# Sliding-window attention and a squared-ReLU FFN: the tail pair moved, squares moved between engines, another order for the first two blocks

## The chip, the cores and the metric

The kernel runs on one core of one Trainium2 chip. The metric is the device time in microseconds of one execution; lower is better. Engines are named as the profile names them: PE (matmuls), DVE (vector), ACT (scalar), POOL (GpSimd) and SP (which only issues DMAs).

## The reference

Attention over 8 batches, 8 heads, 576 positions and a head size of 64, in which each position sees itself and the 63 before it, and behind it an FFN with a squared ReLU on the 4608 tokens:

```python
scores = scale * np.matmul(q, k.transpose(0, 1, 3, 2))
rel = pos[:, None] - pos[None, :]
mask = (rel >= 0) & (rel < 64)
attn = softmax(np.where(mask, scores, -1e9))
x = np.matmul(attn, v)                     # to [4608, 512]
h = np.maximum(x @ w_in, 0.0)              # w_in  [512, 2048]
out = h * h @ w_out                        # w_out [2048, 512]
```

Inputs and output are float32 in device memory.

## The kernel before

**Tiles, pairs, blocks.** Tokens are worked on in 36 tiles of 128, 18 pairs of tiles and 9 blocks of two pairs (512 tokens). A sequence of 576 positions is two pairs of 256 and a rest of 64. The rests of the eight sequences are put together into two special pairs, four rests in each: `TAILS` says which pair numbers these are, and `place` turns the other pairs into sequence and position. A tail pair is loaded by `fetch_tail` (L163): twelve DMAs on SP, the keys and values with the 64 positions ahead of each rest, so twice the bytes of a usual pair; two tiles of keys are transposed for it instead of one. A usual pair is loaded by `fetch_two` with six DMAs.

**One tile of attention.** `S_` makes the scores on PE (L425), `expo` the exponentials on ACT (L431), `keep` applies the mask on DVE as a minimum (L436), `V` multiplies with the values on PE (L448), `norm` divides on DVE (L456, L457). The result x is transposed to xT, by PE and a copy (`X`, `copy_xT`) for blocks 0 to 3, by DMA for later ones. Keys and queries of pairs 0 to 6 are transposed on PE (`T`, L373) and copied out of PSUM by `copy_kT` and `copy_qT`; those of later pairs by DMA (L397).

**The FFN of one block.** `UP(g, f)` (L526) makes one sixteenth of the hidden units of block g: four matmuls into a PSUM bank of `ps_up`, which has two buffers. ACT takes the relu out of the bank (L530), and the square into h2 is made on ACT from the relu alone (L533) if f is in `SQ_ACT`, else on DVE from the bank and the relu (L536). In blocks 0 and 1 the same is done by pairs: `U` (L498), `relu` (L506 on ACT, L508 on DVE), `square` (L517, L519). The output product of block 0 is plain (`O`, L574); that of the later blocks (`out_seven`) uses seven products of half blocks instead of eight (L614), with sums of halves of h2 on DVE (`hsum`, L602) and sums of the weights (`w_out_sum`, L555 to L561).

**What sets the order.** Every engine works its queue in the order in which the program issues. For blocks 0 and 1 that order is written out by hand in `FIRST`, a list of words: `fk`, `fq`, `fv`, `fw`, `fo` fetch keys, queries, values and weights; `kc`, `qc`, `vc` cast them; `vd` copies values to the tile with the halves exchanged; `Tk`, `Tq` transpose, `ck`, `cq` copy the transposed tiles; `w` scales w_in, `o` casts w_out; `S`, `e` (or `ea`, `eb` by halves), `m`, `V`, `n`, `X`, `x` are attention; `U`, `r`, `s` the up-projection of a pair, its relu and square; `O`, `oe`, `st` the output of block 0; `ws` the weight sums; `Wn` issues n matmuls that compute nothing and keep PE busy. A letter after the slash gives the engine (A for ACT, D for DVE, P for POOL) in place of the word's own.

From block 2 on, a stage g puts together the seven products of block g-1, the sixteen `UP` of block g, the attention of block g+1 and the loads of pairs 2g+4 and 2g+5, each with a place between 0 and 1 within the stage, and issues them sorted by it. `later(n, ...)` puts an instruction off by n steps.

Of the kernel before, what the change touches and what calls it, by code (L numbers as in the profile page):

```python
# [12 lines left out]
ALU = mybir.AluOpType  # L13


SQ_ACT = (0, 2, 4, 6, 8, 10, 12, 14)
FIRST = '''
fv3 fk0 fk1 W9 vc3 fq0 kc0/D kc1/A fq1 h0 vd3/D Tk0 W3 kc3/A kc2 fv1 ck0 Tk1 W8 qc0 qc1/D fv0 h2
ck1 Tq0 W11 fv2 cq0 qc2/A fw3 qc3/D S0 fw2 vc1/D fw1 S1 W5 ea0 fw0 vc0/D eb0 vd0/D ea1 vc2 vd1/D
V0 eb1 Tq1 vd2 n0 cq1/A V1 W3 n1 X0 W3 x0 X1 S3 x1/A w3.0 w3.3/A fq2 w3.1 S2 w3.2 ea3 eb3 U0.6 ea2  # L20
V3 eb2 U0.7 n3 w2.1/A w2.3/A w2.0 V2 w2.2 r0.6 X3 n2 U0.5 r0.7 s0.6/A s0.7 X2 U0.4 x2/A x3 w1.0/P
r0.5/D U1.4 r0.4 h4 s0.5 fk2 w1.3/A U1.7 w1.1/P r1.4/D s0.4/A U1.6 w1.2 s1.4/A r1.7/D U1.3 w0.3/A
w0.2 s1.7/A U1.2 w0.0 fv4 r1.6 w0.1 U1.5 r1.3 s1.6 r1.2 qc4 fv5 U0.2 r1.5 s1.2 qc5 s1.3/A s1.5 fk3
kc4 kc5/A Tq2 r0.2 Tk2 vc4 fq3 cq2/A U0.1 ck2/D vd4 U1.1 r0.1 fq4 s0.2 vc5 s0.1/A S4 r1.1/D S5 vd5
e4 U0.0 h6 e5 U0.3 kc7 m4 fv6 r0.0 m5 V4 s1.1/A qc7 fv9 V5 n4 r0.3 U1.0 qc6 s0.0/A n5 fq5 X4 qc8
qc9/A Tq3 x4 r1.0 kc6 X5 s0.3 Tq4 fv7 x5/A vc6 Tk3 s1.0 cq3/A U2.5 vd6 ck3/D fk4 cq4/A U2.0 r2.5/D
S7 r2.0/D S6 e7 U2.2 fv8 s2.5 fo0 vc9/A U2.7 s2.0 e6 vc7 m7 fo1 U2.1 vd7 fo2 r2.2 m6 fo3 U2.4 qc10
s2.2/A h8 r2.1/D qc11/A kc9 V7 V6 r2.7 n7 vc8 U2.3 s2.7/A vd9 n6 s2.1/A U2.6 r2.3 r2.4/D kc8 X7 X6
x7 Tq5 s2.4/A vd8 x6 Tk4 s2.3/A r2.6/D U3.7 ck4 s2.6 o2 U3.6 o0 cq5 r3.7 fv10 o1 s3.7/A S9 S8 r3.6
U3.0 s3.6/A U3.2 e9 r3.0/D o4 U3.4 o7 s3.0/A m9 o3 e8 U3.1 r3.2/D U3.3 s3.2/A m8 o10 r3.1 h10  # L30
r3.4/D O0.0 o5 fv15 s3.1 s3.4/A o6 V8 V9 o8/A O2.0 n9 o9/A fk5 O3.0 n8 o15 o12/A o14/A o11 fk6
O0.1 ws0.0 vc10/A ws0.1 X9 o13/A h12 O3.1 vd10 r3.3/D fv14 ws0.2 X8 O3.2 ws1.1 ws0.3 O0.2 kc10
kc11/A x9 ws1.0 s3.3/A O2.1 ws1.3 fv12 ws1.2 ws2.3 O3.3 x8 fq6 ws2.2 kc12 kc13/A Tk5 ws2.0 O2.2
vc15/A ws2.1 fv11 vc14/A ck5/D Tk6 O0.3 vd14 ck6 fv13 O2.3 oe0 st0 vc12 S11 vd15 oe2/D st2 S10 e11
U3.5 qc13 fkq14 qc12 e10 O1.0 m11 vc11 O1.1 r3.5 m10 vd11 Tq6 vc13 V10 cq6/A V11 vd12 n10 O1.2
fkq15 n11 O1.3 qc14 s3.5 X10 kc14 oe1 st1 X11 x10 oe3 st3 vd13 x11 kc15 qc15
'''


# [1 line left out]
def kernel(  # L41
# [10 lines left out]
    B, H, S, D = q.shape  # L52
    NT, DM = out.shape
    DFF = moe_w_in.shape[1]
    P = 128
    HP = H // 2
    NCK = NT // P
    TAILS = (8, 15)
    W_SCALE = 100.0
    OUT_SCALE = 1.0 / (W_SCALE * W_SCALE)  # L60
    BIG = 65504.0
# [24 lines left out]
    def later(n, fn):  # L86
        if n == 0:
            fn()
        else:
            put_off.append([n, fn])  # L90

    def tick():
        for e in list(put_off):
            e[0] -= 1
            if e[0] <= 0:
                put_off.remove(e)
                e[1]()
# [6 lines left out]
    def is_tail(i):  # L104
        return i // 2 in TAILS

    def place(i):

        p = i // 2 - sum(i // 2 > t for t in TAILS)
        return p // 2, p % 2 * 256 + i % 2 * P  # L110

    def tail_seq(i):

        return 4 * TAILS.index(i // 2) + i % 2 * 2

    def is_first(i):
        return not is_tail(i) and place(i)[1] == 0
# [147 lines left out]
    def copy(eng, out, in_, scale=1.0):  # L265
        if eng is nc.scalar:
            nc.scalar.activation(out=out, in_=in_, func=AF.Copy, scale=scale)  # L267
        elif scale == 1.0:
            eng.tensor_copy(out=out, in_=in_)  # L269
        else:  # L270
            eng.tensor_scalar(out=out, in0=in_, scalar1=scale, scalar2=None, op0=ALU.mult)
# [25 lines left out]
    def shift_v(i, eng=nc.gpsimd):  # L297
        v_ev, v_od, v_next = v_evs[i % NV], v_ods[i % NV], v_ods[(i + 1) % NV]
        copy(eng, v_od[64:P, :, 0:D], v_ev[0:64, :, 0:D])
        if i >= 2 * TAILS[0] and is_first(i):  # L300
            eng.memset(v_od[0:64, :, 0:D], 0.0)
# [9 lines left out]
    def xT_of(g):  # L311
        if g not in xTs:
            xTs[g] = xtp.tile([P, 4, DMC, P], FP16, name="xT", tag="xT")
        return xTs[g]
# [84 lines left out]
    def dma_k(p):  # L399
        if p in TAILS:  # L400
            for i in (2 * p, 2 * p + 1):
                kTs["tail", i] = attw.tile([P, 2, HP, P], FP16, name="kT", tag="kT", bufs=4)
                flip(kTs["tail", i][:].rearrange("p n a t -> p (n a) t"),
                     k16s["tail", i][:].rearrange("p n h d -> p (n h d)"))
        else:
            flip(kT_of(p)[:].rearrange("p a (n t) -> p (a n) t", n=2),
                 k16s[p][:].rearrange("p n h d -> p (n h d)"))
# [76 lines left out]
    def h2_of(g):  # L484
        if g not in h2s:
            h2s[g] = h2pool.tile([P, FFC, 512], FP16, name="h2", tag="h2")
        return h2s[g]
# [35 lines left out]
    def UP(g, f):  # L523
        hps = ps_up.tile([P, 512], FP32, name="hps", tag="ps_u")
        for c in range(DMC):
            nc.tensor.matmul(  # L526
                hps[:], w_in_sb[:, c, f * P:(f + 1) * P], xT_of(g)[:, :, c, :],
                start=(c == 0), stop=(c == DMC - 1))
        hrelu = hrp.tile([P, 512], FP32, name="hrelu", tag="hrelu")
        nc.scalar.activation(out=hrelu[:], in_=hps[:], func=AF.Relu)  # L530
        if f in SQ_ACT:

            later(2 if f == 0 else 0, lambda: nc.scalar.activation(  # L533
                out=h2_of(g)[:, f, :], in_=hrelu[:], func=AF.Square))
        else:
            nc.vector.scalar_tensor_tensor(  # L536
                out=h2_of(g)[:, f, :], in0=hps[:], scalar=0.0, in1=hrelu[:],
                op0=ALU.max, op1=ALU.mult)
        tick()
# [208 lines left out]
    def load(p, part):  # L748

        if p in TAILS:  # L750
            for nm in part:
# [42 lines left out]
    for g in range(2, NTB + 1):  # L794
        if g == 2:
            for k0 in range(0, KH, 2):
                w_out_sum(k0, 3)
        ev = even(out_seven(g - 1))
        if g < NTB:
            ev += [(0.05 + 0.95 * t, s) for t, s in even([lambda f=f: UP(g, f) for f in range(FFC)])]  # L800
        if g + 1 < NTB:
            ev += attention(g + 1)
            ev += loads(2 * g + 3)
        for _, s in sorted(ev, key=lambda e: e[0]):
            s()
# [32 lines left out]
```

The softmax here doesn't subtract the row's maximum and nothing guards it: scores larger than these inputs give would overflow.

## Time and profile before

| | us |
|---|---|
| median of 4 runs (lowest, highest) | 297.52 (296.29, 298.33) |
| the profiled execution | 297.73 |
| its span, first to last instruction | 295.9 |
| PE, DVE, ACT, POOL busy in it | 284.2, 218.0, 189.7, 118.1 |

The profile is of one execution. Its span is 1.8 us shorter than the time of the same execution. Busy times of PE are those of pipelined matmuls, so they overlap; a matmul's own time is longer than the distance to the next one. "Idle before" is the time an engine stood before an instruction, put down to what came last. Times on the timeline are counted from the first instruction.

### The profile page before, as it was taken

How to read it: one execution, taken by the hardware profiler on the slowest of the kernel's cores; microseconds unless marked ns; L12 is line 12 of the kernel's file. 1: busy time of each engine (PE TensorE's matmuls, PEld its weight loads, DVE VectorE, ACT ScalarE, POOL GpSimd, SP SyncE). 2: the span in 40 equal slices, each digit the busy share in tenths (PEclk: the TensorE clock that was granted, in tenths of full speed). 3: DMA queues.
4: the chain of work that ended last, by engine and by line, in shares of the span. 5: the costliest groups of instructions: out<-in, count | busy, mean ns of one | idle time of the engine just before them, and what ended most of it. 6: DMA issues, size and time to landing. Idle time of an engine off the chain costs nothing.

```text
span 295.9 us, 7475 instructions
## 1 busy us (share of the span) xinstructions
PE 284.2 (96%) x3042; PEld 196.7 (66%) x3042; DVE 218.0 (74%) x396; ACT 189.7 (64%) x300; POOL 118.1 (40%) x172
## 2 busy tenths in 40 slices
PE   4999999999989999999999999999999999999995
PEld 3668888755656666666666666666666566666684
DVE  4569798798889569685978587768776976645393
ACT  2688999885574756757675767575757575566500
POOL 2306979558506264545364626232366300000000
PEclk9999999999999999999999999999999999999999
DMA  7999999796699999868895999989999801300133
GB/s 216 297 381 312 305 285 370 215 267 163 183 187 237 190 279 214 191 154 253 197 218 132 232 209 200 149 195 199 228 227 313 120 3 35 144 0 2 71 106 109
DMA packets 151842, 57.64 MB, mean 195 GB/s; under 512 B 128256, under 2 KB 143616, under 8 KB 151808
## 3 DMA queue, kind: packets, MB, share of 16 engines
q1 hardware_dynamic: 151808, 57.16, 79.8%
q8 instruction: 24, 0.39, 0.5%
q14 instruction: 10, 0.08, 0.1%
HBM read 38.80 MB, written 9.44 MB: 163 GB/s over the span
## 4 chain that ended last, share of the span: by engine, by line
PE 73%; DVE 14%; ACT 7%; DMA 2%; issue 2%; SPq 0%; POOL 0%
PE hps L526 30%; PE opsC L614 9%; PE opsD L614 8%; PE hps L498 5%; PE opsA L614 5%; PE opsB L614 5%; DVE hs_all L602 4%; PE av L448 3%; ACT pm L431 2%; PE sc L425 2%; DVE pm L436 2%; DMA k_st<-in_k_dram 2%; ACT h L517 1%; DVE x_sb L457 1%; ACT hrelu L506 1%
## 5 line engine op out<-in xcount | busy, mean ns | idle before, releaser
L526 PE MATMUL hps<-xT,w_in_sb 128*128 128x512 f16 x448 | 112.8, 379 | 2.4 <-DVE h L536 2.4
L530 ACT ACTIVATE hrelu<-hps 128x512 f32<-128x512 f32 x112 | 66.7, 598 | 69.8 <-PE hps L526 68.7
L614 PEld LDWEIGHTS <-h 128*128 128x128 f16 x624 | 60.4, 98 | 20.7 <-issue 0.2
L526 PEld LDWEIGHTS <-w_in_sb 128*128 128x128 f16 x448 | 42.5, 98 | 35.0 <-issue 2.7
L536 DVE SCALAR_TENSOR_TENSOR h<-hps,hrelu 128x512 f16<-128x512 f32 x56 | 38.6, 690 | 29.2 <-ACT hrelu L530 28.8
L269 POOL COPY v_od<-v_ev 64x512 f16<-64x512 f16 x51 | 38.7, 758 | 7.3 <-ACT v_ev L267 3.5
L431 ACT ACTIVATE pm<-sc 128x1024 f16<-128x1024 f32 (+1 forms) x40 | 35.3, 937 | 3.6 <-PE sc L425 3.5
L533 ACT ACTIVATE h<-hrelu 128x512 f16<-128x512 f32 x56 | 35.2, 629 | 1.6
L614 PE MATMUL opsA<-w_out_sb,h 128*128 128x256 f16 x240 | 31.0, 273 | 0.0
L614 PE MATMUL opsD<-wb_all,h 128*128 128x256 f16 x240 | 30.9, 273 | 0.0
L614 PEld LDWEIGHTS <-hs_all 128*128 128x128 f16 x256 | 25.0, 98 | 8.6
L498 PE MATMUL hps<-xT,w_in_sb 128*128 128x256 f16 x256 | 30.2, 273 | 0.0
L498 PEld LDWEIGHTS <-w_in_sb 128*128 128x128 f16 x256 | 24.2, 98 | 3.0
L457 DVE TENSOR_TENSOR x_sb<-av,rden 128x512 f16<-128x512 f32 x36 | 24.9, 692 | 1.2
L436 DVE TENSOR_TENSOR pm<-pm,mask_inner 128x1024 f16<-128x1024 f16 x25 | 19.3, 772 | 6.5 <-ACT pm L431 6.4
L269 POOL CAST k<-kq_st 128x512 f16<-128x512 f32 x18 | 11.8, 657 | 27.1 <-DMA kq_st<-in_k_dram 26.6
L269 POOL CAST q<-kq_st 128x512 f16<-128x512 f32 x22 | 14.8, 673 | 18.4 <-DMA kq_st<-in_q_dram 18.3
L269 POOL CAST v_ev<-kq_st 128x512 f16<-128x512 f32 x16 | 11.2, 701 | 20.1 <-DMA kq_st<-in_v_dram 15.8
L636 DVE SCALAR_TENSOR_TENSOR osb_all<-opsD,u 128x512 f32<-128x512 f32 x14 | 9.7, 691 | 11.3 <-PE opsD L614 11.3
L614 PE MATMUL opsC<-w_out_sb,h 128*128 128x256 f16 x128 | 16.4, 273 | 0.0
L614 PE MATMUL opsB<-wb_all,hs_all 128*128 128x256 f16 x128 | 16.4, 273 | 0.0
L614 PE MATMUL opsC<-w_out_sb,hs_all 128*128 128x256 f16 x128 | 16.4, 273 | 0.0
(102 smaller groups left out, 379.3 us busy)
## 6 DMA issues: line engine op xcount, KB each, us to landing
kq_st<-in_k_dram SPq DMA_DIRECT2D x26, 256.0 KB, 3.7
kq_st<-in_v_dram SPq DMA_DIRECT2D x24, 256.0 KB, 3.8
out_dram<-osb_all SPq DMA_DIRECT2D x12, 512.0 KB, 4.1
kq_st<-in_q_dram SPq DMA_DIRECT2D x18, 256.0 KB, 4.4
v_st<-in_v_dram SPq DMA_DIRECT2D x16, 256.0 KB, 5.3
k_st<-in_k_dram SPq DMA_DIRECT2D x7, 512.0 KB, 5.6
q_st<-in_q_dram SPq DMA_DIRECT2D x7, 512.0 KB, 5.7
out_dram<-osb_all SPq DMA_DIRECT2D x11, 256.0 KB, 2.8
```

What stands on the lines that cost most here:

```text
L269: eng.tensor_copy(out=out, in_=in_)
L431: nc.scalar.activation(out=pms[i][:, part], in_=scs[i][:, part], func=AF.Exp, scale=1.0 / float(D) ** 0.5)
L436: nc.vector.tensor_tensor(out=pms[i][:, part], in0=pms[i][:, part], in1=mask[:].rearrange("p (o a) r -> p o (a r)", o=1) .to_broadcast([P, ...
L457: nc.vector.tensor_tensor(out=xs[i // 2][:, i % 2], in0=avs[i][:, :, :, 0:D], in1=rden[:].to_broadcast([P, 2, 4, D]), op=ALU.mult)
L498: nc.tensor.matmul(hps[:, f, :], w_in_sb[:, c, (2 * j + f) * P:(2 * j + f + 1) * P], xT_of(p // 2)[:, n0:n0 + 2, c, :], start=(c == 0), st ...
L526: nc.tensor.matmul(hps[:], w_in_sb[:, c, f * P:(f + 1) * P], xT_of(g)[:, :, c, :], start=(c == 0), stop=(c == DMC - 1))
L530: nc.scalar.activation(out=hrelu[:], in_=hps[:], func=AF.Relu)
L533: later(2 if f == 0 else 0, lambda: nc.scalar.activation(out=h2_of(g)[:, f, :], in_=hrelu[:], func=AF.Square))
L536: nc.vector.scalar_tensor_tensor(out=h2_of(g)[:, f, :], in0=hps[:], scalar=0.0, in1=hrelu[:], op0=ALU.max, op1=ALU.mult)
L602: nc.vector.tensor_tensor(out=Sh[i][:, ks], in0=x[:, ks], in1=y[:, ks], op=op)
L614: nc.tensor.matmul(rows_of(bank, m), a[:, kk, m * P:(m + 1) * P], w[:, kk], start=(first and kk == 0 and (m == 0 or bank in apart)), stop= ...
L636: nc.vector.scalar_tensor_tensor(out=dst, in0=banks[bank][:, ms], scalar=OUT_SCALE, in1=sums[add][:, ms], op0=ALU.mult, op1=ALU.add)
```

## The change

Three things change besides the list `FIRST`. The first tail pair becomes pair 10 (the first of block 5) instead of pair 8 (the first of block 4). `SQ_ACT` holds f=1 in place of f=2, so the square of f=1 goes to ACT and that of f=2 to DVE in every block from 2 on. In block 2, f=2 and f=9 are made on ACT too: ten squares there and six on DVE. The list `FIRST` holds the same steps in another order and with other engines for some of them; its `W` words add up to 43 matmuls in place of 42.

```diff
--- before.py
+++ after.py
@@ -13,27 +13,27 @@
 ALU = mybir.AluOpType
 
 
-SQ_ACT = (0, 2, 4, 6, 8, 10, 12, 14)
+SQ_ACT = (0, 1, 4, 6, 8, 10, 12, 14)
 FIRST = '''
-fv3 fk0 fk1 W9 vc3 fq0 kc0/D kc1/A fq1 h0 vd3/D Tk0 W3 kc3/A kc2 fv1 ck0 Tk1 W8 qc0 qc1/D fv0 h2
-ck1 Tq0 W11 fv2 cq0 qc2/A fw3 qc3/D S0 fw2 vc1/D fw1 S1 W5 ea0 fw0 vc0/D eb0 vd0/D ea1 vc2 vd1/D
-V0 eb1 Tq1 vd2 n0 cq1/A V1 W3 n1 X0 W3 x0 X1 S3 x1/A w3.0 w3.3/A fq2 w3.1 S2 w3.2 ea3 eb3 U0.6 ea2
-V3 eb2 U0.7 n3 w2.1/A w2.3/A w2.0 V2 w2.2 r0.6 X3 n2 U0.5 r0.7 s0.6/A s0.7 X2 U0.4 x2/A x3 w1.0/P
-r0.5/D U1.4 r0.4 h4 s0.5 fk2 w1.3/A U1.7 w1.1/P r1.4/D s0.4/A U1.6 w1.2 s1.4/A r1.7/D U1.3 w0.3/A
-w0.2 s1.7/A U1.2 w0.0 fv4 r1.6 w0.1 U1.5 r1.3 s1.6 r1.2 qc4 fv5 U0.2 r1.5 s1.2 qc5 s1.3/A s1.5 fk3
-kc4 kc5/A Tq2 r0.2 Tk2 vc4 fq3 cq2/A U0.1 ck2/D vd4 U1.1 r0.1 fq4 s0.2 vc5 s0.1/A S4 r1.1/D S5 vd5
-e4 U0.0 h6 e5 U0.3 kc7 m4 fv6 r0.0 m5 V4 s1.1/A qc7 fv9 V5 n4 r0.3 U1.0 qc6 s0.0/A n5 fq5 X4 qc8
-qc9/A Tq3 x4 r1.0 kc6 X5 s0.3 Tq4 fv7 x5/A vc6 Tk3 s1.0 cq3/A U2.5 vd6 ck3/D fk4 cq4/A U2.0 r2.5/D
-S7 r2.0/D S6 e7 U2.2 fv8 s2.5 fo0 vc9/A U2.7 s2.0 e6 vc7 m7 fo1 U2.1 vd7 fo2 r2.2 m6 fo3 U2.4 qc10
-s2.2/A h8 r2.1/D qc11/A kc9 V7 V6 r2.7 n7 vc8 U2.3 s2.7/A vd9 n6 s2.1/A U2.6 r2.3 r2.4/D kc8 X7 X6
-x7 Tq5 s2.4/A vd8 x6 Tk4 s2.3/A r2.6/D U3.7 ck4 s2.6 o2 U3.6 o0 cq5 r3.7 fv10 o1 s3.7/A S9 S8 r3.6
-U3.0 s3.6/A U3.2 e9 r3.0/D o4 U3.4 o7 s3.0/A m9 o3 e8 U3.1 r3.2/D U3.3 s3.2/A m8 o10 r3.1 h10
-r3.4/D O0.0 o5 fv15 s3.1 s3.4/A o6 V8 V9 o8/A O2.0 n9 o9/A fk5 O3.0 n8 o15 o12/A o14/A o11 fk6
-O0.1 ws0.0 vc10/A ws0.1 X9 o13/A h12 O3.1 vd10 r3.3/D fv14 ws0.2 X8 O3.2 ws1.1 ws0.3 O0.2 kc10
-kc11/A x9 ws1.0 s3.3/A O2.1 ws1.3 fv12 ws1.2 ws2.3 O3.3 x8 fq6 ws2.2 kc12 kc13/A Tk5 ws2.0 O2.2
-vc15/A ws2.1 fv11 vc14/A ck5/D Tk6 O0.3 vd14 ck6 fv13 O2.3 oe0 st0 vc12 S11 vd15 oe2/D st2 S10 e11
-U3.5 qc13 fkq14 qc12 e10 O1.0 m11 vc11 O1.1 r3.5 m10 vd11 Tq6 vc13 V10 cq6/A V11 vd12 n10 O1.2
-fkq15 n11 O1.3 qc14 s3.5 X10 kc14 oe1 st1 X11 x10 oe3 st3 vd13 x11 kc15 qc15
+fv3 fq0 h0 fk0 W9 fq1 qc0/A qc1 fk1 vc3 Tq0 W1 vd3/D kc0/A kc1/D fv0 cq0/A Tk0 W6 ck0/D qc3/A fv1
+fv2 S1 kc2/A S0 qc2/A vc0/D fw3 ea1 h2 vd0 kc3/D Tq1 W8 fw2 eb1 fw1 ea0 fw0 eb0 h4 Tk1 vc1/D vd1
+V0 W6 ck1 n0 cq1/A vc2 V1 X0 W6 n1 x0/A vd2/D X1 S2 x1/A S3 W7 fk2 w3.2 w3.1/A w3.0 ea2 w3.3 eb2
+U0.7 ea3 eb3 V2 U0.6 w2.0/A n2 w2.2/A w2.1 V3 r0.6 w2.3 X2 s0.6/A n3 U0.5 r0.7 x2 X3 s0.7/A U0.4
+x3 fq2 w1.0/A w1.1 U1.7 r0.5/D r0.4 s0.5 s0.4/A U1.6 r1.7 w1.2 w1.3 U1.4 fv4 r1.6 s1.7 U1.2 s1.6
+r1.4 kc4 w0.0/A w0.1 fv5 U1.3 w0.2/A s1.4 U1.5 r1.3 r1.2/D qc4 kc5/A U0.2 fq3 s1.2 s1.3/A w0.3 Tk2
+qc5/A fq4 r1.5/D U1.1 vc4 r0.2 s1.5 vd4 Tq2 ck2/D U0.1 cq2/A fk3 vc5 r1.1/D vd5 r0.1 S4 s0.2 S5
+fv7 e4 s1.1 qc7 U0.0 s0.1 e5 qc8 fv6 U1.0 m4 qc9 r0.0 m5 fv9 V4 r1.0 kc7 qc6/A n4 V5 s1.0/A U0.3
+n5 s0.0/A fq5 Tq3 kc6/A X5 X4 fk4 r0.3 x5 Tq4 vc6 x4 s0.3/A Tk3 h6 vd6 cq3 U2.5 ck3 fv13 U2.0 vc7
+cq4 r2.5 vc9 s2.5/A S7 S6 r2.0/D vd7 fv8 U2.7 e6 s2.0 fo0 U2.1 fo1 r2.7/D e7 kc9 m6 U2.4 fo2 vd9
+r2.1 fo3 m7 s2.1/A U2.6 s2.7/A kc8 r2.4/D qc11/A V7 qc10 V6 r2.6 h8 n7 vc13 U2.3 s2.6/A n6 s2.4/A
+X7 U2.2 x7/A r2.3 X6 Tk4 s2.3/A x6 Tq5 r2.2/D U3.0 fk5 cq5/A o3 s2.2 o1 U3.6 ck4/D r3.0 o0 U3.2
+vc8/A r3.6 vd8 U3.3 r3.2/D s3.0/A s3.2 S9 r3.3 vd13 S8 s3.6 e9 U3.5 s3.3 o6 U3.4 e8 m9 o5 U3.7
+o2/A fv14 m8 o4 r3.5 U3.1 r3.7/D s3.5/A o7 V9 r3.4 o9 V8 s3.7/A s3.4 o8 O0.0 fv10 o11/A o15 n9
+O1.0 o10/A o13 fk6 r3.1 X9 o14 O2.0 s3.1/A x9 kc11 fv11 n8 o12/A O1.1 vc14 kc10/A h10 ws0.2 O1.2
+vc10 ws0.3 fv12 X8 O0.1 x8 ws1.2 kc13 O2.1 ws0.0 fq6 vd10 ws1.0 O2.2 fv15 vd14 Tk5 ws2.2 O2.3 ck5
+vc11 O3.0 ws0.1 kc12/A vd11 ws1.3 S10 fkq14 S11 ws2.3 e10 qc13 O3.1 ws1.1 qc12 oe2 st2 O0.2 m10
+vc15 e11 h12 Tk6 vc12 O0.3 ck6 m11 vd15 fkq15 O3.2 ws2.1 vd12 oe0/D st0 V10 V11 kc14 O3.3 n11 qc14
+Tq6 n10 O1.3 cq6/A ws2.0 X10 X11 oe1 st1 qc15 x11 oe3 st3 x10 kc15
 '''
 
 
@@ -55,7 +55,7 @@
     P = 128
     HP = H // 2
     NCK = NT // P
-    TAILS = (8, 15)
+    TAILS = (10, 15)
     W_SCALE = 100.0
     OUT_SCALE = 1.0 / (W_SCALE * W_SCALE)
     BIG = 65504.0
@@ -528,7 +528,7 @@
                 start=(c == 0), stop=(c == DMC - 1))
         hrelu = hrp.tile([P, 512], FP32, name="hrelu", tag="hrelu")
         nc.scalar.activation(out=hrelu[:], in_=hps[:], func=AF.Relu)
-        if f in SQ_ACT:
+        if f in SQ_ACT or g == 2 and f in (2, 9):
 
             later(2 if f == 0 else 0, lambda: nc.scalar.activation(
                 out=h2_of(g)[:, f, :], in_=hrelu[:], func=AF.Square))
```

## The prediction, made before the change was run

> **What bounds the kernel now.** I read the page's first lines, then the waits of PE, the windows by stage, and last the timelines of DVE and ACT at the places where PE stood.
>
> ```profile
> span 295.9 us, 7475 instructions
> PE 284.2 (96%) x3042; PEld 196.7 (66%) x3042; DVE 218.0 (74%) x396; ACT 189.7 (64%) x300; POOL 118.1 (40%) x172
> L526 PE MATMUL hps<-xT,w_in_sb 128*128 128x512 f16 x448 | 112.8, 379 | 2.4 <-DVE h L536 2.4
> ```
>
> PE is the bound, and at full rate: in the chain of waits four up-projection matmuls (L526) take 0.86 us, 215 ns each, back to back, for most of the span. The last number is the opening: PE stood 2.4 us in all because the square on DVE (L536) gave its PSUM bank back late.
>
> ```profile
> PE hps L526 <- DVE h L536: 2.4, 4, 0.9
> ```
>
> The windows are one per stage (start:end, stretch, busy us and instructions by engine, clock, DMA share, GB/s):
>
> ```profile
> 20.15:57.40 37.25, 36.57 (x527) 31.65 (x522) 31.48 (x56) 35.35 (x58) 26.64 (x38) 1.00 1.02 310
> 77.20:109.20 32.00, 30.78 (x356) 20.44 (x354) 25.04 (x45) 19.57 (x33) 13.81 (x21) 1.00 1.02 217
> 109.20:138.10 28.90, 28.90 (x307) 19.11 (x306) 21.91 (x37) 19.05 (x32) 14.89 (x22) 1.00 0.85 201
> 195.90:225.60 29.70, 29.04 (x306) 19.24 (x307) 21.91 (x35) 19.15 (x32) 14.23 (x21) 1.00 1.15 228
> ```
>
> Blocks 3, 4 and 5 run at 28.9 us with PE full: nothing to win there. Block 2 (second row) lasts 32.0, blocks 6 and 7 last 29.7. In the first stage (first row) ACT is busy 35.35 of 37.25, so ACT is nearly as tight as PE. The first up-projection starts at 20.15; 20 us of start-up lie before it.
>
> Now the stall of block 6, on DVE:
>
> ```profile
> 196.89 1.06 DVE L436 TENSOR_TENSOR pm<-pm,mask_inner 128x1024 f16<-128x1024 f16 x1 [0.22 <-ACT pm L431]
> ...
> 201.63 0.98 DVE L602 TENSOR_TENSOR hs_all<-hs_all,h 128x1024 f16<-128x1024 f16 x1
> 202.53 0.68 DVE L536 SCALAR_TENSOR_TENSOR h<-hps,hrelu 128x512 f16<-128x512 f32 x1
> ...
> 204.95 0.69 DVE L536 SCALAR_TENSOR_TENSOR h<-hps,hrelu 128x512 f16<-128x512 f32 x1
> ```
>
> DVE never rests from 196.89 to 205.64. The square at 202.53 is that of f=1; PE, ready for f=3 at about 202.6, starts at 203.26. The square at 204.95 is f=3's: keep it in mind. And the same place in block 5, where PE does not stand:
>
> ```profile
> 171.97 0.69 DVE L602 TENSOR_TENSOR hs_all<-hs_all,h 128x1024 f16<-128x1024 f16 x1
> 172.58 0.68 DVE L536 SCALAR_TENSOR_TENSOR h<-hps,hrelu 128x512 f16<-128x512 f32 x1
> 173.61 0.21 DVE L456 RECIPROCAL rden<-av 128x8 f32<-128x8 f32 x1 [0.35 <-PE av L448]
> ```
>
> **What the Trainium skill says.** "Perfetto Trace Analysis", Identifying the Most-Contended Engine, holds matmul busy time for a poor measure of the headroom; the trace agrees: a mean of 379 ns stands for a spacing of 215. "SBUF — State Buffer", Who interferes with whom: a DVE instruction with two SBUF inputs contends with a GpSimd instruction that reads SBUF, one with a single SBUF input does not, and ACT waits for nobody. The trace agrees: the half sums (L602) and the mask minimum (L436) take 0.68 alone and 0.98 to 1.09 while POOL casts run (195.3 to 202.1), while the square, which reads PSUM and one SBUF tile, takes 0.68 in both. "ScalarE: Activation LUTs", Rules for kernel authors, sends simple operations to VectorE. For these float32 operands the trace differs: 629 ns on ACT (L533), 690 on DVE (L536). "TensorE: Matmul & The Clock Gate", Back-to-back issue gap: columns / 2.4 GHz + 2.5 ns, 109 for 256 columns, as eight of opsA in 0.87 us show; an estimate from it for the one more warm-up matmul (43 for 42) is 0.11 us, inside start-up waits, so nothing.
>
> **The change, part by part.**
>
> *Second square to ACT.* f=1 goes to ACT and f=2 to DVE, in blocks 2 to 8: one square of 629 for one of 690 on each, and the totals hold. An ACT square reads only hrelu, so the bank is free after the relu. In block 6 that is at 200.24 (relu of f=1), and the wait of 0.75 (PE left V at 202.5) for f=3 is gone. What is late next: f=2's square now stands where f=1's stood, ends at 203.2, and f=4 needs that bank at about 203.5: no wait. But f=5 needs f=3's bank, and f=3's square still ends at 205.64, since DVE has the same work before it. PE, ahead by 0.63, would reach f=5 at 205.23 and waits until 205.69 against 205.86 today. So I count 0.17 for block 6, not 0.75; block 7 has the same picture (square ends at 235.35, f=5 starts at 235.57), 0.17 again. Bounds: 0 to 1.5 for both. In blocks 3 to 5 DVE has 0.35 of rest after this square: nothing.
>
> *Two more in block 2.* Both f=1 and f=2 are on ACT there. Today DVE runs without rest through the last weight sums (2.73) and half sums and ends f=1's square at 84.91; f=3 starts at 84.96 and could at 83.93: 1.03. ACT takes two more squares just then: exponentials to 82.92, then relu, square, relu, square, the evacuation p (L629), each 0.5 to 0.6 apart. The relus of f=1 and f=2 end near 83.4 and 84.4, before f=3 (83.93) and f=4 (84.8) want the banks; f=3's relu waits behind the evacuation until about 85.4, its square on DVE ends near 86.7, f=5 wants it at 87.2. So the full 1.03 goes. f=9: at 98.75 its square stands on DVE behind two minima that wait for exponentials, and PE waits 0.5 for f=11 (99.48). On ACT the bank is free at 98.59: 0.5 goes. Bounds 0.5 to 1.6 together.
>
> *Tail pair from 8 to 10.* All that it issues moves from block 2's stage to block 3's. On SP twelve loads and three transposes for the six and two of a usual pair (those of today run from 83.76 to 99.60); on POOL two casts of 1.04, two of 0.67 and four of 0.74 to 0.83, 6.6 us, against 7.1 for a usual pair; on DVE no kh copies (0.26 + 0.34) for it; two stores per half block for one. On SP pair 11's loads and the stores stand behind it, on POOL pair 11's casts. DMA: block 3 is at 0.85 of 28.9, 24.6 us; four loads more at 0.94 (landing every 0.94 from 87.46) and a transpose of 0.82 make 29.2, just full, as block 2's is now; block 4 at 0.83 takes the rest. Its scores are wanted only a half stage later. One memset on POOL (0.52) goes. I take +0.1, bounds -0.3 to +1.5: casts that slip into the start of blocks 4 and 5 slow DVE there by the 0.75 of block 6 each.
>
> *First order, start.* Loads go q, k, q, k instead of k, k, q, q; the same bytes lie before w_in, so its last quarter lands at 17.91 as now. With q0 and k0 first (5.45 and 7.52 by today's landings), scores need: cast 0.6, transpose 0.45, copy 1.3, thus about 10 instead of 12.75; xT of pair 0 is then copied near 17.6, today at 19.12. Then the weights bind: 17.91, casts of 0.42 in a row on DVE with one exponential half and one cast on ACT, first up-projection near 19.1: -1.05. Bounds 0 to -1.2.
>
> *First order, the rest.* After the first unit both orders hold the same PE work (32 units, 16 product steps, T, S, V, X). Gone is the wait for pair 5's keys:
>
> ```profile
> 69.36 1.23 DVE kT L269
> ...
> 70.63 0.64 PE sc L425 x32
> ```
>
> This copy queued on DVE behind the weight sums; now it is on ACT, two product steps (1.73) ahead of the scores: -0.8. Other stalls between 20.15 and 68 were about 2.1 in sum (the longest 0.69 near 37). The new order makes its own: quarter 2 (lands 20.63) for the third unit, 0.2 to 0.6; pair 2's cq on ACT (1.33) with one unit (0.87) before S4, 0.5; V5 behind two exponentials, 0.4. ACT has 61 instructions for 57 from the first unit to the first product, 35.35 x 61 / 57 = 37.8 us for some 38.6. I take +0.6 against today, bounds -1 to +4.
>
> Sum: -0.34 - 1.53 + 0.1 - 1.05 - 0.8 + 0.6 = **-3.0**. The profiled execution took 297.73 (span 295.9 and 1.8 around it), so 294.7; the median of the runs, 297.52, lies 0.2 under it, so 294.5.
>
> **Rivals.**
>
> 1. The early start is not carried: PE starts at 19.1, but weights and pairs land as before and it waits again. Then the first stage gains nothing: -0.34 - 1.53 + 0.1 = -1.8, 295.7. For it: DMA share 1.02 up to 57. Against: POOL and DVE use the pairs after 27 us several us after landing.
> 2. Slower: ACT's queue binds the first stage. Place: from the first unit to the first product. Its idle 1.9 us is waiting for PE and can't be filled, so the four more instructions cost 2.4, and four late handovers (cq, ck, kc in front of T or S) 0.69 each, as the longest today: +5.2, with no early start. 5.2 - 1.8 = +3.4: 300.9. It decides from a first-stage loss of 3.3 us on. Against it: ACT had rests of 0.2 to 0.4 to the end.
> 3. The squares don't do it: ACT, already busy at 81 to 85, frees banks as late as DVE did, and the first order comes out level with a start worth 1.0: 296.5.
>
> **How the numbers follow.** Forecast 0.62 (293 to 296); rival 1 0.20; rival 2 0.08; rival 3 0.10. A measurement of this kernel tells about 0.5% (1.5 us) from no change, so faster is below 296.0. Forecast 0.95 and rival 1 0.75 of their chance, rival 3 0.4: 0.78; slower: rival 2, 0.08; the rest 0.14. The range 292.8 to 297.4 takes in the larger gain in blocks 6 and 7 and, above, rivals 1 and 3.
>
> **What would show it.** First up-projection near 19.1; PE waiting for L536 under 1.5 us in all, with none in block 2 and short ones before f=5 in blocks 6 and 7; pair 5's scores without a wait for kT; block 2 near 30.4; block 3 still 28.9; DMA share of block 3 near 1.0. The forecast is wrong if the first product of block 1 (opsA) starts later than 77.2, or if blocks 4 and 5 grow by over 0.5.

## The result and the profile after

The changed kernel takes 296.40 us (median of 43 executions) beside 297.35 for the kernel before (64 executions). The ratio is 0.9968, 95% interval 0.9958 to 0.9979: 0.95 us faster, where 3.0 had been forecast. A second measurement of the same kernel gave 0.9969 (0.9951 to 0.9987). Below, a time has the number of executions behind it in brackets, and a ratio, always to the kernel before measured beside it, its 95% interval.

The page of the profile after: its span, the busy times of the engines, and the group of the up-projections.

```profile
span 295.1 us, 7478 instructions
PE 284.7 (96%) x3043; PEld 196.6 (67%) x3043; DVE 211.9 (72%) x391; ACT 192.7 (65%) x304; POOL 115.8 (39%) x172
L526 PE MATMUL hps<-xT,w_in_sb 128*128 128x512 f16 x448 | 112.9, 379 | 0.4 <-DMA xT<-x_sb 0.3
```

The idle time in front of the up-projections was 2.4 us behind the square on DVE (L536). It is 0.4 now, and most of that is a transfer (xT) that was not in this line before. PE's waits in the same profile say it too:

```profile
PE hps L526 <- DMA xT<-x_sb: 0.3, 1, 0.3
PE sc L425 <- ACT qT L267: 0.5, 1, 0.5
PE av L448 <- ACT kT L267: 0.3, 1, 0.3
```

So 2.0 us of stalls went, but the time fell by half of that. The windows by stage, cut at the same times as those of before (start:end, stretch, busy us and instructions of PE, its weight loads, DVE, ACT and POOL, clock, DMA share, GB/s):

```profile
20.15:57.40 37.25, 36.41 (x539) 31.10 (x531) 31.55 (x59) 34.77 (x59) 19.25 (x31) 1.00 1.05 322
77.20:109.20 32.00, 32.00 (x367) 21.35 (x366) 23.57 (x47) 22.12 (x36) 15.39 (x22) 1.00 0.76 169
109.20:138.10 28.90, 28.90 (x307) 19.10 (x305) 19.92 (x36) 19.17 (x31) 8.84 (x11) 1.00 1.00 207
```

PE is now full in block 2 as well (32.00 of 32.00), ACT is not fuller in the first stage (34.77), and the DMA share has moved from block 2 (0.76) to block 3 (1.00), as forecast. What went the other way lies at the start. This is the chain of waits from the last transpose of keys to the first up-projection (start, us, what):

```profile
15.67 0.46 PE kT_ps L373 x8
16.13 0.02 issue
16.16 1.31 ACT kT L267
17.47 1.17 ACT qT L267
18.64 0.45 ACT xT L267
...
21.17 0.87 PE warm L545 x7
22.04 0.87 PE hps L498 x8
```

On the timeline the first up-projection starts at 21.88; before it was 20.15, and 19.1 had been forecast. No weight binds here (the casts of the quarter of w_in that is used first end at 20.7): a chain of copies on ACT does, and then seven matmuls that compute nothing (`W7`).

To compare kernels I measure each profile at three kinds of places: the first up-projection (U), the first product of block 1 (opsA, which opens the stage of block 2), and from opsA to opsA for the later blocks.

| profile | first U | U to opsA | block 2 | blocks 3, 4, 5 | block 6 | block 7 |
|---|---|---|---|---|---|---|
| before | 20.15 | 57.02 | 31.98 | 28.91, 28.88, 28.87 | 29.66 | 28.88 |
| after | 21.88 | 56.45 | 30.59 | 28.91, 29.35, 28.87 | 29.16 | 28.27 |
| after, second profile | 20.98 | 56.63 | 30.59 | 28.91, 29.05, 28.87 | 28.95 | 28.65 |

### The profile page after: what moved, and what is told of

It reads as the page before. It is cut to its first block, busy times and chain, and to the rows that moved or that the text cites. A ratio compares the mean times of both kernels' runs of the same rounds, so it can differ in the third digit from the quotient of the medians.

```text
span 295.1 us, 7478 instructions
## 1 busy us (share of the span) xinstructions
PE 284.7 (96%) x3043; PEld 196.6 (67%) x3043; DVE 211.9 (72%) x391; ACT 192.7 (65%) x304; POOL 115.8 (39%) x172
## 4 chain that ended last, share of the span: by engine, by line
PE 85%; DVE 7%; DMA 4%; ACT 2%; issue 1%; SPq 0%
PE hps L526 31%; PE opsC L614 10%; PE opsD L614 8%; PE opsA L614 8%; PE hps L498 6%; PE ops L574 5%; PE opsB L614 4%; PE av L448 3%; PE sc L425 3%; DMA k_st<-in_k_dram 2%; DVE h L519 2%; DMA xT<-x_sb 1%; PE xt_ps L468 1%; DVE hs_all L602 1%; PE kT_ps L373 1%; PE warm L545 1%
## 5 line engine op out<-in xcount | busy, mean ns | idle before, releaser
L614 PEld LDWEIGHTS <-h 128*128 128x128 f16 x624 | 60.5, 98 | 20.7 <-issue 0.2
L536 DVE SCALAR_TENSOR_TENSOR h<-hps,hrelu 128x512 f16<-128x512 f32 x54 | 37.2, 690 | 33.2 <-ACT hrelu L530 33.0
L533 ACT ACTIVATE h<-hrelu 128x512 f16<-128x512 f32 x58 | 36.5, 629 | 1.6
L436 DVE TENSOR_TENSOR pm<-pm,mask_inner 128x1024 f16<-128x1024 f16 x25 | 20.2, 809 | 5.6 <-ACT pm L431 5.5
```

Of the source, the lines that this page charges most:

```text
L436: nc.vector.tensor_tensor(out=pms[i][:, part], in0=pms[i][:, part], in1=mask[:].rearrange("p (o a) r -> p o (a r)", o=1) .to_broadcast([P, ...
L533: later(2 if f == 0 else 0, lambda: nc.scalar.activation(out=h2_of(g)[:, f, :], in_=hrelu[:], func=AF.Square))
L536: nc.vector.scalar_tensor_tensor(out=h2_of(g)[:, f, :], in0=hps[:], scalar=0.0, in1=hrelu[:], op0=ALU.max, op1=ALU.mult)
L614: nc.tensor.matmul(rows_of(bank, m), a[:, kk, m * P:(m + 1) * P], w[:, kk], start=(first and kk == 0 and (m == 0 or bank in apart)), stop= ...
```

## The experiments

**The three parts one by one.** Each part was done alone, and each was undone, which leaves the pair of the other two.

```diff
 sq_only    before with:  SQ_ACT = (0, 1, 4, ...);  if f in SQ_ACT or g == 2 and f in (2, 9):
 first_new  before with:  FIRST of the changed kernel
 tail_only  before with:  TAILS = (10, 15)
 first_old  after with:   FIRST of before            (squares and tail left)
 tail_old   after with:   TAILS = (8, 15)            (list and squares left)
 first_tail after with:   SQ_ACT and `if` of before  (list and tail left)
```

Squares alone:

> The kernel before with the new engines for the squares alone (f=1 on ACT, f=2 on DVE, in block 2 f=2 and f=9 on ACT too); old list, old tail pair. My prediction gave the squares 1.5 us in block 2 and 0.34 in blocks 6 and 7: ratio 0.994. The traces so far say 0.5 to 1.0 in block 2 and 0.2 each in 6 and 7: 0.996. Rival, the squares do nothing: 1.000, block 2 at 31.4 to 32.0 still.

Measured 295.45 (6 executions), 0.9925 (0.9901 to 0.9949).

The list alone:

> The kernel before with the changed list FIRST, old squares, old tail pair. By the ledger the new list alone costs: start +1.7, rest of the first stage -0.6, so +1.1 us (ratio 1.004), with the stalls of 1.0 and 0.5 in block 2 still there. Rival, the new list is worth its gain once it isn't held up by the other edits: 0.998 or lower.

Measured 296.35 (15), 0.9953 (0.9932 to 0.9974).

The tail alone:

> The kernel before with the tail pair at pair 10 and nothing else. If the tail pair costs what the profiles show (0.5 to 0.8 us ahead of block 4) and wins at most 0.3 in block 2, the ratio is 1.000 to 1.002. Rival: relieved DMA in block 2 pays for it, 0.998.

Measured 298.19 (22), 1.0009 (0.9991 to 1.0027).

List taken back:

> The changed kernel with the list FIRST of the kernel before: only the squares and the tail pair are new. If the ledger of the two traces adds up, the squares win 1.4 us in block 2 and 1.1 in blocks 6 and 7, the tail pair loses 0.5, and with the old start the kernel takes about 2.0 us less than before (ratio 0.993), 1.1 less than the changed one. First up-projection at 20.2, first opsA of block 1 at 77.2. Rival: the blocks' gains came from the later start (loads further ahead of PE); then this is near 0.998.

Measured 295.84 (9), 0.9927 (0.9897 to 0.9957): faster than with the new list.

Tail taken back:

> The changed kernel with the tail pair back at pair 8. If the wait of 0.45 us at the start of block 4 comes from the tail pair's loads and transposes on SP ahead of the transposes of x, it is gone and the kernel takes 0.5 us less than the changed one (0.995 of before). Rival: DMA is full in block 2 again and the stall comes back there or at the start of block 3, so no difference from the changed kernel (0.997) or a loss.

Measured 295.83 (15), 0.9942 (0.9920 to 0.9963): 0.0026 less than with the tail at 10, though the two intervals touch.

Squares taken back:

> The changed kernel with the squares of the kernel before: new list and new tail pair. If list and squares overlap (with the new list the stall ahead of f=3 in block 2 is 0.3 us, not 1.0, since POOL no longer slows the weight sums), the squares are worth only 0.8 in block 2 and 0.3 in blocks 6 and 7 here, so this is 1.0 us above the changed kernel: ratio 1.000. Rival: the parts add, then 2.0 above it: 1.003.

Measured 298.09 (22), 1.0021 (1.0002 to 1.0039): without the squares the other two parts make the kernel slower than before.

With before (1) and after (0.9968) these are all eight combinations. The effect of a part is read four times, on each combination of the other two, in units of the time before:

| part | alone | beside the others | mean of four |
|---|---|---|---|
| squares | -0.0075 | -0.0011 on the list, -0.0082 on the tail, -0.0053 on both | -0.0055 (-1.6 us) |
| list | -0.0047 | +0.0017 on the squares, +0.0012 on the tail, +0.0041 on both | +0.0006 (+0.2 us) |
| tail | +0.0009 | +0.0068 on the list, +0.0002 on the squares, +0.0026 on both | +0.0026 (+0.8 us) |

Each ratio is known to about 0.002, so each mean to about 0.5 us. The squares win, the tail loses on the mean, mostly through the combination with the list alone, and the list wins only where it stands alone.

**The second measurement.** The changed kernel, unaltered.

> The changed kernel unaltered, for a second profile of it and for its time beside the others of this call. If its first profile caught a slow start (first up-projection 21.88) and the others of the same list (19.5, 20.3) are as usual, the first up-projection lies between 19.4 and 21 here. Rival: the changed kernel's start is always near 21.9, and the others owe theirs to their edits.

Ratio 0.9969; but its profile has the first U at 20.98 instead of 21.88. One profile does not settle where the start lies.

**Only the beginning of the old list.**

```diff
-fv3 fq0 h0 fk0 W9 fq1 qc0/A ... S2 x1/A S3 W7 fk2 ... U0.7
+fv3 fk0 fk1 W9 vc3 fq0 kc0/D ... X1 S2 x1/A w3.0 w3.3/A fk2 w3.1 S3 w3.2 ea2 eb2 h4 U0.7
```

> The changed kernel whose list FIRST begins as the one before does, up to the first up-projection (tiles 2 and 3 swapped so that the rest fits), and goes on with the changed list. If the lost time is in the start alone: first up-projection at 20.2, opsA of block 1 at about 76.7, 1.7 us less than the changed kernel (0.991 of before). Rival: the data after w_in come at the same times whatever the start, so PE waits for them later and only part, under 0.6 us, is won.

296.00 (22), 0.9947 (0.9925 to 0.9969), first U at 21.23. The new beginning, worth 1.05 us in the prediction, is not faster than the old one; by the ratios (0.9968 and 0.9947) it is 0.6 us slower, within the noise.

**PE kept busy earlier.**

```diff
-fv3 fq0 h0 fk0 W9 fq1 ... Tq0 W1 vd3/D ...
+fv3 fq0 h0 fk0 W17 fq1 ... Tq0 W6 vd3/D ...
```

> The changed kernel with more warm-up matmuls while PE waits for the first loads: W17 for W9 in front of the first transpose and W6 for W1 behind it. In the profile of the changed kernel the four matmuls of 512 columns ahead of scores 1 and 0 stand 1.53 us apart by pairs, in that of first_new 0.87: the clock of PE. If the cold clock costs the start, the pairs stand 0.87 apart here, the first up-projection is at 19.5 to 20.3, and the median falls 0.5 to 1.0 us under the changed kernel's 296.4. Rival: the start is set by loads (k0 and the first quarter of w_in vary by 1 us and more from execution to execution), so the pairs come closer and nothing is won.

294.93 (6), 0.9910 (0.9885 to 0.9935), first U at 19.27: 1.5 us faster than the changed kernel by the medians, 1.7 by the ratios. The reason is seen on PE's timeline, in the fills of 128x512 that open the scores of tiles 1 and 0. After:

```profile
10.90 1.06 PE L417 MATMUL sc<-osb_all,ident 128*128 128x512 f16 x2
12.43 1.03 PE L417 MATMUL sc<-osb_all,ident 128*128 128x512 f16 x2
```

The kernel with the new list alone (the last two lines are `W7` and the first up-projection, for later):

```profile
10.03 0.60 PE L417 MATMUL sc<-osb_all,ident 128*128 128x512 f16 x2
10.90 0.61 PE L417 MATMUL sc<-osb_all,ident 128*128 128x512 f16 x2
18.70 0.94 PE L545 MATMUL warm<-mask_first,ident 128*128 128x256 f16 x7
19.47 1.04 PE L498 MATMUL hps<-xT,w_in_sb 128*128 128x256 f16 x8
```

And warm_early, with the additional fillers:

```profile
9.09 0.59 PE L417 MATMUL sc<-osb_all,ident 128*128 128x512 f16 x2
```

The same two matmuls take 1.06 in one execution and 0.60 in the other, and the scores follow 1.53 us after one another instead of 0.87. The lists are the same word for word. By these durations PE ran at about half its rate up to some 14.5 us in after, and up to some 10 us with the new list alone. Of eight profiles with the new beginning and its own fillers ahead of these scores five have the slow fill (not the list alone, and not no_w7 and w7_to_w1 below); of the four with the additional fillers (warm_early, and three more below) none has. From the first transpose of keys (L373) to the first U it took 12.30 to 13.09 in those five, 11.55 with the list alone, and 11.30 in warm_early. So half rate costs 0.8 to 1.5 us of the start. It is not all of the scatter: of the 2.41 us between the first U of after and that with the list alone, 0.87 lie before this transpose, which waits for keys that landed later. The page's row of the granted clock does not show the half rate; it reads the same in both kernels:

```profile
PEclk9999999999999999999999999999999999999999
```

The old list has this too: its `W11` took 1.20 us in the profile of before and 2.03 in first_old, start to next start. "TensorE: Matmul & The Clock Gate", Part 1 of the Trainium skill (the HAM clock gate), says that the array runs at half clock until it has been active for some 3.4 us, and that the window is free-running, so that one kernel starts differently from run to run. The traces agree with the half rate and with the difference from run to run (1.06 and 0.60); no run here measures the 3.4 us.

**The filler in front of the first up-projection taken out, or cut to one.**

```diff
 no_w7:      S3 W7 fk2  ->  S3 fk2
 w7_to_w1:   S3 W7 fk2  ->  S3 W1 fk2
```

> The changed kernel without W7, the seven warm-up matmuls between the scores of tile 3 and the first up-projection. If they stand on the path, the first up-projection follows the scores at once, 0.77 us earlier, and the median falls by up to 0.8 us. Rival: the casts of w_in's last quarter, or the second quarter's arrival at the third unit, take the time over: under 0.3 us.

296.43 (22), 0.9960 (0.9940 to 0.9979): nothing won over the changed kernel, though the first U starts at 19.24. Its chain to the first U runs through the weights:

```profile
10.52 7.88 DMA hs_all<-in_moe_w_in_dram
18.39 0.02 issue
18.42 0.78 DVE w_in_sb L271 x2
```

So the limit that the prediction named is there, close behind the copies and the filler. The gain at the start comes back later: first U to opsA takes 57.95 instead of 56.45. Here is PE's wait of no_w7 at the products of block 1:

```profile
PE opsA L614 <- ACT osb_all L267: 0.5, 1, 0.5
```

This is 0.5 of the 1.5; the rest is not traced. Each `W` word takes a PSUM tile in turn from two pools. Taking one word out shifts the turn of every tile behind it, and opsA then got a bank that ACT empties late. This is a property of the program. So the cleaner experiment keeps one matmul:

> W7 ahead of the first up-projection cut to W1. Unlike in no_w7 the warm-up still takes one PSUM tile, so all later tiles keep their place in the turn between the two pools (without it the first opsA waited 0.7 us for a bank that ACT emptied late). If W7 is on the path, first up-projection 0.65 us sooner than in the changed kernel's executions with the same arrival of weights, no wait at the first opsA, and up to 0.6 us won. Rival: the first stage gives it back (waits for w_in's quarters and between 32 and 38), nothing won.

295.09 (5), 0.9916 (0.9889 to 0.9943), some 1.3 to 1.5 us faster than the changed kernel by medians and by ratios. PE's timeline:

```profile
18.39 0.28 PE L545 MATMUL warm<-mask_first,ident 128*128 128x256 f16 x1
18.51 1.04 PE L498 MATMUL hps<-xT,w_in_sb 128*128 128x256 f16 x8
```

Seven matmuls hold the first U for 0.77 (18.70 to 19.47 above), one for 0.12. That explains 0.65 of it. The rest is not shown: this profile is one at full rate (its first fill takes 0.59), and five executions may have had kind starts.

Both ideas together with the old place of the tail:

> The changed kernel with the early warm-up matmuls, without W7 and with the tail pair at pair 8: the three supposed losses mended together. If they add: 0.7 + 0.7 + 0.5, so 294.5 (ratio 0.990). Rival: start and rest are tied by the loads, then no better than tail_old (0.994).

295.33 (11), 0.9925 (0.9896 to 0.9953), first U at 18.19, but again 57.73 to opsA, and a new wait of 1.6 for a transpose of xT at the start of block 7. `W7` was taken out whole here as well. The 294.5 that was expected did not come, and there is no gain over warm_early.

**The transpose behind the tail's loads.** SP issues in program order. SP's DMAs of after, in front of block 4:

```profile
130.85 1.98 SPq L121 DMA_DIRECT2D kq_st<-in_k_dram  x2
132.87 1.80 SPq L121 DMA_DIRECT2D kq_st<-in_q_dram  x2
134.76 2.32 SPq L477 DMA_TRANSPOSE xT<-x_sb  x1
```

The same transpose in before:

```profile
131.44 1.23 SPq L477 DMA_TRANSPOSE xT<-x_sb  x1
```

And the chain of waits of after at the same place:

```profile
134.76 4.36 DMA xT<-x_sb
139.12 0.05 issue
139.17 1.04 PE hps L526 x4
```

The second xT transpose of block 4 stands behind the four loads of pair 11, which stand behind the tail pair. It was issued at 131.44 in before and landed at 134.17, in good time; now it lands at 139.12, and PE waits for it. The experiment puts pair 11's loads behind it:

```diff
-ev.append((t + 0.14, lambda a=a, x=kq: load(a + 1, x)))
+ev.append((t + (0.29 if a == 10 else 0.14), lambda a=a, x=kq: load(a + 1, x)))
```

> The changed kernel with the keys and queries of pair 11 issued behind the transposes of x for block 4's second half, not ahead of them: an exchange of four loads and one transpose on SP, no other change. If PE's wait at the start of block 4 (0.45 to 1.5 us in the five profiles with the tail pair at 10) is the place of that transpose in SP's queue, block 3 to 4 falls from 29.3 and more to 28.9 and 0.5 to 0.8 us are won. Rival: DMA bandwidth is full there, the transpose lands as late, and nothing changes.

SP in that kernel:

```profile
131.38 1.26 SPq L477 DMA_TRANSPOSE xT<-x_sb  x1
132.70 1.21 SPq L121 DMA_DIRECT2D kq_st<-in_k_dram  x2
```

It lands at 134.75 and block 4 takes 28.97. 295.91 (7), 0.9940 (0.9911 to 0.9969): 0.8 us better than the changed kernel by the ratios, as much as the tail cost on average, but the interval overlaps that of the changed kernel. The profiles show the wait in block 4 gone and no more than that: from the first opsA of block 1 to that of block 8 it took 175.11 here, 175.15 and 175.02 in the two profiles of after, whose waits for this transpose were short (below).

**What was found, together.** warm_early with xt_ahead:

> The changed kernel with the early warm-up matmuls (W17, W6) and the exchange on SP of xt_ahead. If both losses are as I think and add, 294.3 to 294.6, ratio 0.989 to 0.990. Rival: warm_early's 294.93 came of few runs and kind starts; then about 295.8.

294.41 (6), 0.9902 (0.9872 to 0.9931). And with `W7` cut to `W1` besides:

> The changed kernel with the three mends together: early warm-up (W17, W6), W1 for W7 ahead of the first up-projection, and pair 11's keys and queries behind the transposes of x. From the single runs (warm_xt 0.9902, w7_to_w1 0.9916): first up-projection near 18.5, blocks 3 to 4 at 28.9, ratio 0.986 to 0.989. Rival: an earlier start is paid back by the waits at pair 2's scores and mask (0.7 and 0.4 to 0.8 us now), then 0.990.

293.95 (6), 0.9884 (0.9837 to 0.9931), the lowest median of all and faster than both kernels; its interval overlaps those of warm_early, w7_to_w1 and warm_xt. Its span is 292.6. This is its chain at the start, to be held against that of after:

```profile
13.10 0.46 PE kT_ps L373 x8
13.56 0.02 issue
13.59 1.32 ACT kT L267
14.90 1.17 ACT qT L267
16.07 0.46 ACT xT L267
...
18.60 0.22 PE warm L545
18.82 0.02 issue
18.84 1.05 PE hps L498 x8
```

The links are the same and as long, 2.57 us earlier (13.10 for 15.67), and the filler is 0.22 for 0.87. The forecast of 19.1 for the first U is kept only by kernels that differ from the changed one: here, in w7_to_w1 (18.51) and in warm_no_w7_tail8 (18.19).

## Why the prediction was wrong

The direction was right and the size was not; the direction came from the squares, for on the mean of the combinations the list and the tail cost time. Two terms of the sum were mis-sized, the start (-1.05) and the tail (+0.1), and two terms were added although they fill the same waits, those of the list and of the squares. The largest term, that of the squares, was right where they stand alone.

**First order, start: -1.05 forecast, no gain seen.** The step "Then the weights bind: 17.91 ... first up-projection near 19.1" failed: in after the copies on ACT and `W7` bind, with PE at half rate, and the first U lies at 21.88. Three things are wrong in the step.

- It took the start of one profile for that of the kernel. The first U with the old beginning lay at 20.15, 20.97, 21.23, 20.57 and 19.79 (mean 20.54), and with the new one, unedited, at 21.88, 20.98, 19.47, 20.32, 20.22 and 20.08 (mean 20.49). By `W11`, PE ran at full rate in two of the five old starts (1.20 in before, 1.19 in tail_only) and at half rate for some of it in three (1.66 to 2.05). In the last six, the last quarter of w_in lands between 16.1 and 18.6; the step assumed 17.91.
- It costed the `W` words at nothing, "inside start-up waits". `W7` stands on the path that sets the first U, 0.77 us.
- It followed the transfers and not the copies. Behind the second pair's transposes stand `ck1`, `cq1` and the copy of xT on ACT, 1.31 + 1.17 + 0.45 = 2.9 us in a row, and V1 waits for the first of them, since it takes that PSUM bank next (the wait for kT, 0.3, in the list above).

The profiled executions with the old beginning were on average 0.8 us longer than the median of their kernel, those with the new one 0.0. If this lies in the start, the usual first U is some 0.8 us later with the new beginning than with the old. This is an estimate; start_old (0.6) speaks for it.

**First order, the rest: -0.2 forecast, -0.55 seen.** From the first U to opsA the profiles with the old list took 57.02 to 57.38, those with the new one, unedited, 56.45 to 56.93. The wait for pair 5's keys is gone. The stalls that were to come instead came, by the trace's waits: 0.5 in front of S4 for the copy on ACT (0.5 forecast), 0.3 to 0.5 in front of V5 (0.4).

**Second squares: -1.87 forecast, -2.2 alone.** With the squares only, the window of block 2 is full:

```profile
77.60:108.00 30.40, 30.40 (x356) 20.44 (x352) 23.48 (x43) 20.45 (x34) 12.74 (x19) 1.00 0.99 210
```

Block 2 goes from 31.98 to 30.44, 1.54 less, where 1.53 was forecast. In block 6 the wait moved from f=3 to f=5, as the working had it. Block 6 of after, on DVE:

```profile
202.75 0.68 DVE L536 SCALAR_TENSOR_TENSOR h<-hps,hrelu 128x512 f16<-128x512 f32 x1
205.03 0.68 DVE L536 SCALAR_TENSOR_TENSOR h<-hps,hrelu 128x512 f16<-128x512 f32 x1
```

and on PE:

```profile
205.77 1.02 PE L526 MATMUL hps<-xT,w_in_sb 128*128 128x512 f16 x4
```

The square of f=3 ends at 205.71, PE starts f=5 at 205.77; 205.69 was forecast. PE stood 0.28 there. For the two blocks 0.34 had been forecast; with the squares alone they won 0.50, block 6 going from 29.66 to 29.49 and block 7 from 28.88 to 28.55. What after has in these blocks (29.16 and 28.27) is not the squares' doing alone: the list alone, with the old squares, has 29.15 and 28.46. "The same picture" did not hold for block 7, which lasted 28.88 before and not the 29.7 of the prediction's opening; PE stood 0.61 before its f=3, and after has no wait in that block.

**The tail: +0.1 forecast, +0.8 measured on average.** The step counted DMAs, casts and bytes, and block 3 stayed at 28.9 with its DMA share at 1.00, as it said. It named "pair 11's loads and the stores" as what stands behind the tail on SP. It did not name what stands behind pair 11's loads: block 4's second transpose of xT. There are nine profiles with the tail at 10 and SP's order left alone: block 4 took 29.05 to 29.74 in seven of them, 30.35 and 30.44 in two, against 28.88 in every profile with the tail at 8. The forecast's own sign of failure was blocks 4 and 5 growing by over 0.5; block 4 grew by 0.47 in the profile of after. Over the nine it grew by 0.70 on average, and that is near the 0.8 of the ratios. In the two profiles of after this wait was short (0.47 and 0.17), and blocks 2 and 6 are 0.2 to 0.4 shorter than in tail_old: from opsA of block 1 to that of block 8 it took 175.15 and 175.02 in after, 175.51 in tail_old. So the wait is shown in every profile, but that the tail costs 0.8 in the changed kernel rests on the ratios alone. There is more when the old squares are kept. PE's waits with list and tail, without the squares:

```profile
PE hps L526 <- DVE h L536: 2.1, 4, 0.6
PE hps L526 <- DMA xT<-x_sb: 1.4, 1, 1.4
```

The casts that come later slow DVE's half sums at the start of block 5 (the last two before the square of f=1 take 1.09 and 0.98, in before 0.68 and 0.69), this square comes late there too, and block 5 grows from 28.87 to 29.57. This the step had priced, as "0.75 of block 6 each", at the upper bound.

**The parts do not add.** The sum treated the 1.03 us before f=3 of block 2 as the squares' alone. The list takes most of it away too. The last four weight sums on DVE in before:

```profile
77.81 2.82 DVE L561 TENSOR_TENSOR w_out_sb<-w_out_sb 128x512 f16<-128x512 f16 x4
```

with the new list alone:

```profile
76.89 1.42 DVE L561 TENSOR_TENSOR w_out_sb<-w_out_sb 128x512 f16<-128x512 f16 x4
```

and the window from 77 to 85, before:

```profile
77.00:85.00 8.00, 7.13 (x83) 4.94 (x81) 7.93 (x14) 6.66 (x11) 3.92 (x6) 1.00 0.87 180
```

with the new list alone:

```profile
77.00:85.00 8.00, 7.86 (x78) 4.79 (x78) 5.96 (x12) 6.39 (x11) 0.00 (x0) 1.00 1.01 210
```

POOL is busy 3.92 us there in before and not at all with the new list. The sums then take half the time, DVE has rest (5.96 of 8), and the stall before f=3 is 0.30 instead of 1.03. That a DVE instruction with two SBUF operands contends with a POOL instruction that reads SBUF is what "SBUF — State Buffer", Who interferes with whom, of the Trainium skill states; the trace agrees with 2.82 against 1.42. So on the list the squares win 0.49 in block 2 (31.40 with the list alone, 30.91 in tail_old), not 1.54. Beyond block 2 it is the same. From opsA of block 1 to that of block 8 the profiles took 177.18 in before, 175.16 with the squares, 175.67 with the list and 175.51 with both: 2.0 and 1.5 alone, 1.7 together. Why the list shortens blocks 6 and 7 was not looked into.

**The rivals.** The early start that is not carried: its premise, a start at 19.1, did not hold, but its mechanism was seen in part. Where the first U came earliest with the pools' turns unchanged, at 18.51 (w7_to_w1) and 18.84 (all_mended), the way to opsA took 57.07 and 57.25, 0.6 to 0.8 longer than in after. ACT's queue as the bound: refuted, ACT is busy 34.77 in the 37.25 us from the first U on (35.35 in before), and the way to opsA got shorter. The squares that do nothing: refuted by sq_only (0.9925).

**What stays open.** The list's effect can be put together from the estimate for the start (+0.8), the way from the first U to opsA, and that from opsA of block 1 to that of block 8. It comes to -1.2 alone (+0.8 - 0.5 - 1.5; measured -1.4), +0.6 on the squares (+0.5), +0.5 on the tail (+0.4) and -0.1 on both (+1.2), each measured value to between 0.6 and 1.0. The first three agree; the last does not. Between their first U and their end the profiles of after are 2.5 us shorter than that of before, and the time is 0.95 shorter; the later start accounts for about half of the difference. A longer wait in block 4 in the executions without a profile would fit (with the same order from the first U on, start_old has 30.35 there, after 29.35), but it is not shown.

## What to carry to other kernels

When an item is moved on an in-order issue queue, list everything that stands behind it until the next item that the bound engine waits for, not only the neighbours; here a transpose that stood four loads further back was what came late. Do not forecast a gain in a start-up from one profile; ask first how far apart the starts of several executions lie. And where two edits aim at the same wait, count the wait once.

## What the runs showed of the hardware that I had not expected

PE's rate in the first 15 us differs between executions of one and the same list: two scores 1.53 or 0.87 us apart, with no trace of it in the page's row of the clock. Thirteen more matmuls that compute nothing, put into PE's early waits, went with a first U at 19.27 and a ratio of 0.9910 instead of 0.9968; a filler that stands on the path costs its full length instead, 0.77 us for seven.
